# Whole 128x128 tiles for the router's flag sums, list products and spreads

## The chip, the cores and the metric

The kernel runs on one core of a Trainium2 chip. The metric is device time in microseconds (us), the median of three runs; a lower number is better. PE is the matrix engine (TensorE), PEld its weight load, DVE the vector engine, ACT the scalar engine, POOL the GpSimd engine, SP the engine that issues most DMAs.

## The reference, cut to what matters

Three layers run one after the other on 2176 tokens (4 batches of 512 local and 32 global positions) of 512 numbers each.

1. Attention, 8 heads of 64; global positions see everything, local ones a window of 32 to either side and the global ones.
2. A dense layer: `g = max(x @ w_in, 0) + alpha * min(x @ w_in, 0)`, then `g @ w_out` (512 to 2048 to 512).
3. A routed layer with 8 experts (512 to 1024 to 512), in which each expert takes exactly 2176 / 8 = 272 tokens. The assignment is greedy over all token and expert pairs:

```
logits = x @ w_gate
for idx in argsort(-logits.flatten()):
    tok, e = idx // 8, idx % 8
    if tok is taken or expert e has 272 tokens: continue
    give tok to e
out[tokens of e] = max(x[tokens of e] @ w1[e], 0) @ w2[e]
```

The change lies in the program of that assignment (the router) alone.

## The kernel before, in words

The three layers follow each other in time. PE's order is written out by hand in the dense layer's second half and in the experts (`manual_schedule`); the other engines' order is made by a planner when the program is built.

The router (`router`, `phase`, `listing`) does not sort. It closes one expert after the other, eight in all: `phase(k)` finds the threshold at which the next expert is full, and `listing(k)` makes the list of its 272 tokens (`IDS`), with which POOL later gathers their rows (`fetch_x`, tile `xg`). Tokens lie as 17 chunks (NT) of 128 partitions.

For seven of the eight experts `phase` takes six rounds. A round goes back and forth between PE and DVE:

- DVE compares the scores with 63 (first two rounds) or 31 thresholds (`against`, tile `gs`, 0 or 1).
- PE counts by thresholds and experts: `pc`, nine matmuls of 128 rows x 128 columns of weights (L886).
- DVE makes `lack` and the flags `sat` (L889, L891): 63 or 31 partitions by 8 experts.
- PE sums the flags over partitions and spreads the sum to all partitions: `pa`, one matmul with `ones` as weights over 63 or 31 rows (L898). This is the flag sum.
- DVE turns the sum into the next thresholds `th` (L901, L910) and goes on with `gs`.

At the end of a phase come `pq` (two matmuls of 128 rows by 128 columns, weights `late` and `ones`) and `pr` (one, weights `ones`, L965). The list of the expert before is made in the gaps of the next one's rounds: DVE builds `va` (tokens' numbers by 17 columns of the list) and `sb` (16 slots, at a pitch of 32), PE multiplies them with two chunks at a time: the list product `pl`, nine matmuls with 48 columns of weights and 68 moving columns (L831). DVE copies the two diagonal blocks to `lb` (L835), and one matmul with 64 rows, the spread `ps` (L838), brings them to all partitions.

PE does not stand still for this. Its matmuls are put between those of the dense layer's last product (`gemm2b`, L1174) and of the experts (`up`, L1047, and `down`, L1063), all in fp32 with 272 moving columns (tiles `h`). How many lie between two router steps is set by the constants WB, WA, WQ, WR and WL, in us of PE work, that the generators yield, and by `advance`, which counts them down. After `gemm2b`, PE gathers the first expert's tokens (`xt`) with filler matmuls (`idle`, L108) between. Expert weights come by DMA in pieces of 0.5 MB (`raw`, three buffers), ACT rounds each (L72) and POOL takes the rest (L73, tile `m`). `hh` and `hl` are the hidden layer in two parts, `xsh` and `xsl` the gathered tokens, `ot` an expert's result, `orow` its rows ahead of the scatter to the output.

Of the kernel before, what the change touches and what calls it, by code (L numbers as in the profile page):

```python
# [9 lines left out]
F32 = mybir.dt.float32  # L10
F32R = mybir.dt.float32r
BF = mybir.dt.bfloat16
# [3 lines left out]
OP = mybir.AluOpType  # L16
# [9 lines left out]
def tile_attention_moe_moe(ctx: ExitStack, tc: tile.TileContext, qkw, vw,  # L26
                           w_in, w_out, gate, w1, w2, out):
    nc = tc.nc
    V, A, P, T = nc.vector, nc.scalar, nc.gpsimd, nc.tensor
    B, H, S, D, SG = BHSDG  # L30
    DM, DF = w_in.shape
    E, _, FF = w1.shape
    NTOK = B * (S + SG)
    NT = NTOK // 128
# [274 lines left out]
    with ExitStack() as at:  # L309
# [299 lines left out]
        c = 0  # L609
# [31 lines left out]
    with tc.tile_pool(name="dc2", bufs=1, side="right") as dc, tc.tile_pool(name="pW", bufs=2, space=PSUM) as pW:  # L641
        more = []
        parts = [(win_part, i) for i in range(2 * KD)] + [(wout_part, i) for i in range(KH)]
        n = 0
# [22 lines left out]
    with ExitStack() as mo:  # L667
# [12 lines left out]
        LB = 16  # L680
# [36 lines left out]
        V.tensor_scalar(own, cols[:, :8].unsqueeze(1).to_broadcast([128, 3, 8]), pq_f[:, 0:1], None, op0=OP.is_equal)  # L717
        fr_b = rc_.tile([128, 128], I32, name="fr_b")
        V.tensor_scalar(fr_b, fr, LB - 1, None, op0=OP.bitwise_and)
        lb = rc_.tile([64, 2, 24], BF, name="lb")  # L720
        V.memset(lb, 0.0)
        spread = rc_.tile([64, 128], BF, name="spread")
        V.tensor_scalar(spread, fr_b[:64], pq_f[:64, 1:2], None, op0=OP.is_equal)
        ones = rc_.tile([128, 128], BF, name="ones")
        V.memset(ones, 1.0)
        one_c = rc_.tile([128, 2 * NT], F32, name="one_c")
# [32 lines left out]
        rp = rc_.tile([128, 2, E], F32, name="rp")  # L759
        V.memset(rp, float(CAP))  # L760
        ohs, gs, gi, vas, sbs = [], [], [0], [], []
        for i in range(2):
            ohs.append(rc_.tile([128, NT + 1, E], BF, name=f"ohs{i}"))
            P.memset(ohs[i], 0.0)
            gs.append(rc_.tile([128, NT + 1, 64], BF, name=f"gs{i}"))
            P.memset(gs[i], 0.0)
            vas.append(rc_.tile([128, NT + 1, LA, 2], BF, name=f"vas{i}"))
            P.memset(vas[i], 0.0)
            sbs.append(rc_.tile([128, NT + 1, 32], BF, name=f"sbs{i}"))
            P.memset(sbs[i], 0.0)  # L770
        Lrow = gx2.tile([128, LR], F32, name="Lrow")
        loadx(0, 1)
# [39 lines left out]
        def listing(k, pos):  # L812
            ra = rt.tile([128, NT], F32, name="ra")
            V.tensor_scalar(ra_h, pos, 1.0 / LB, -0.5 - 0.5 / LB, op0=OP.mult, op1=OP.add)
            V.tensor_scalar(ra, ra_h, MR, -MR, op0=OP.add, op1=OP.add)
            rb = rt.tile([128, NT], F32, name="rb")
            V.scalar_tensor_tensor(rb, ra, -float(LB), pos, op0=OP.mult, op1=OP.add)
            yield WL
            ha = rt.tile([128, NT, LA], BF, name="ha")
            V.tensor_tensor(ha, ra.unsqueeze(2).to_broadcast([128, NT, LA]),  # L820
                            col_h.unsqueeze(1).to_broadcast([128, NT, LA]), op=OP.is_equal)
            va, sb = vas[k % 2], sbs[k % 2]
            V.tensor_tensor(va[:, :NT], ha.unsqueeze(3).to_broadcast([128, NT, LA, 2]),
                            idc.unsqueeze(2).to_broadcast([128, NT, LA, 2]), op=OP.mult)
            yield WL
            V.tensor_tensor(sb[:, :NT, :LB], rb.unsqueeze(2).to_broadcast([128, NT, LB]),
                            slots.unsqueeze(1).to_broadcast([128, NT, LB]), op=OP.is_equal)
            yield WL
            pl = pm.tile([32 + LB, 2, LA, 2], F32, name="pl", tag="sm")
            for c in range(0, NT, 2):  # L830
                T.matmul(pl.rearrange("p c a t -> p (c a t)"), sb[:, c:c + 2].rearrange("p c l -> p (c l)")[:, :32 + LB],  # L831
                         va[:, c:c + 2].rearrange("p c a t -> p (c a t)"), start=c == 0, stop=c + 2 > NT)
            for i in range(2):
                r = slice(32 * i, 32 * i + LB)
                V.tensor_copy(lb[r, :, :LA], pl[r, i].rearrange("p a t -> p t a"))  # L835
            yield WL
            ps = pm.tile([128, 2, 3, 8], F32, name="ps", tag="sm")
            T.matmul(ps.rearrange("p t q a -> p (t q a)"), spread, lb.rearrange("p t a -> p (t a)"), start=True, stop=True)  # L838
            pk = rt.tile([128, 2, 3, 8], F32, name="pk")
            V.tensor_tensor(pk, ps, own.unsqueeze(1).to_broadcast([128, 2, 3, 8]), op=OP.mult)  # L840
            with nc.allow_low_precision(reason="whole numbers below 4096"):
                V.tensor_reduce(IDS[:, k], pk.rearrange("p t q a -> p q t a"), axis=AX.XY, op=OP.add)
            listed[0] = k + 1
            V.tensor_scalar(TT[:, :, k], ps[:, :, 2, 0], own[:, 0, k:k + 1], None, op0=OP.mult)
            if k == E - 1:
                with nc.allow_low_precision(reason="whole numbers below 4096"):
                    V.tensor_reduce(TID, TT.rearrange("p t e -> p (t e)"), axis=AX.X, op=OP.add)
# [22 lines left out]
        def phase(k, prev, v, mx, g):  # L870
# [8 lines left out]
            if not last:  # L879
                cur = None  # L880
                for i, s in enumerate(SH):
# [5 lines left out]
                                 ohw[:, c:c + 2].rearrange("p a e -> p (a e)"), start=c == 0, stop=c + 2 > NT)  # L887
                    lack = rt.tile([64, E], F32, name="lack")
                    V.tensor_tensor(lack[:n - 1], pc[64:63 + n, 1], rp[64:63 + n, 1], op=OP.subtract)  # L889
                    sat = rt.tile([64, E], BF, name="sat")  # L890
                    V.scalar_tensor_tensor(sat[:n - 1], pc[:n - 1, 0], -1.0, lack[:n - 1], op0=OP.mult, op1=OP.is_le)  # L891
                    if cur is not None:
                        n2 = (TH + [1])[i + 1]
# [1 line left out]
                        V.tensor_tensor(base[:, :n2], jt[i + 1], cur[:, 0:1].to_broadcast([128, n2]), op=OP.bitwise_xor)  # L895
                    yield WA[i]
                    pa = pm.tile([128, 64], F32, name="pa", tag="sm")
                    T.matmul(pa[:, :E], ones[:n - 1, :], sat[:n - 1], start=True, stop=True)  # L898
                    sj = sj_h
                    nf = rt.tile([128, 1], F32, name="nf")  # L900
                    V.tensor_scalar(sj, pa[:, :E], MF, 0.0, op0=OP.add, op1=OP.max, accum_out=nf)  # L901
# [463 lines left out]
```

## Time and profile before

| | |
|---|---|
| median of 3 runs | 867.75 us (864.87 to 870.67) |
| profiled execution | 866.48 us, its span 864.7 us |
| PE | busy 820.0 us (95%), 8380 matmuls |
| DVE | busy 467.2 us (54%) |
| ACT | busy 389.7 us (45%) |
| POOL | busy 348.6 us (40%) |
| chain that ended last | PE 73%, DVE 8%, issue 7%, ACT 5%, DMA 4%, POOL 3% |
| mean granted PE clock | 0.979 |

A share is an average over the whole span. The router's matmuls all start between 490 and 760 us, so it is there that the profile has to be read: by stretches, by the waits of PE inside them, and by the start times of single matmuls. A matmul's row gives its start and its length through the pipeline; since matmuls overlap, what one costs is seen in the distance between starts.

### The profile page before, as it was taken

The numbers are of one execution on the slowest core, as the hardware profiler recorded it, in microseconds if no ns is written. First come the engines' busy times: TensorE is split into PE (matmuls) and PEld (weight loads), VectorE is DVE, ScalarE is ACT, GpSimd is POOL, SyncE is SP. The second block draws the span as 40 slices with busy tenths as digits, with TensorE's granted clock in tenths as the row PEclk, the third lists the DMA queues.
The fourth block names the chain that finished last, engine by engine and source line by source line (L and its number), as shares of the span: only waits on it lengthen the run. The fifth ranks groups of instructions, "written<-read, shape, count | busy, mean of one in ns | idle before, by whom it ended". The sixth has DMA issues, their size and how long they took to land.

```text
span 864.7 us, 21014 instructions
## 1 busy us (share of the span) xinstructions
PE 820.0 (95%) x8380; PEld 748.4 (87%) x8380; DVE 467.2 (54%) x1654; ACT 389.7 (45%) x970; POOL 348.6 (40%) x299
## 2 busy tenths in 40 slices
PE   5789999999988999999999999999899999999995
PEld 3668788988988999898989899998689999899995
DVE  6789955364388734143333466766576776722120
ACT  5677656474455543332322434341254544454431
POOL 1124322020245534200000638370598868779601
PEclk9869999999999999999999999999999999999998
DMA  8965742631345302202211227242366655556300
GB/s 343 361 237 167 266 152 77 213 126 47 107 149 172 101 27 79 72 7 64 93 54 51 79 65 257 65 136 71 93 205 210 173 173 166 170 181 185 110 25 37
DMA packets 47993, 115.99 MB, mean 134 GB/s; under 512 B 4183, under 2 KB 20951, under 8 KB 45847
## 3 DMA queue, kind: packets, MB, share of 16 engines
q1 hardware_dynamic: 44999, 105.73, 37.9%
q0 software_dynamic: 2896, 8.92, 3.1%
q8 instruction: 66, 1.08, 0.5%
q14 instruction: 32, 0.26, 0.1%
HBM read 96.80 MB, written 17.83 MB: 133 GB/s over the span
## 4 chain that ended last, share of the span: by engine, by line
PE 73%; DVE 8%; issue 7%; ACT 5%; DMA 4%; POOL 3%; SPq 1%; POOLq 0%; ACTq 0%; DVEq 0%
PE h L191 20%; PE h L1174 12%; PE y L222 9%; PE h L1047 8%; PE h L1063 7%; PE o L422 3%; DVE mag L90 2%; PE lp L279 2%; DMA qk<-in_qk_dram 2%; PE go L471 2%; PE s L385 2%; POOL m L73 1%; PE t L411 1%; DMA raw<-in_moe_w_dram 1%; PE idle L108 1%
## 5 line engine op out<-in xcount | busy, mean ns | idle before, releaser
L191 PE MATMUL h<-xh,win 128*128 128x272 f32 x768 | 165.0, 298 | 3.5 <-DVE g L197 1.9
L73 POOL TENSOR_TENSOR m<-raw,m 128x1024 fp32r<-128x1024 f32 x64 | 152.3, 2403 | 22.0 <-ACT m L72 21.6
L191 PEld LDWEIGHTS h<-xh,win 128*128 128x128 f32 x768 | 126.5, 190 | 11.7 <-issue 4.1
L73 POOL TENSOR_TENSOR glo<-g,ghi 128x272 fp32r<-128x272 f32 x64 | 56.8, 890 | 142.8 <-ACT ghi L72 142.7
L222 PE MATMUL y<-ghi,wout 128*128 128x272 f32 x512 | 112.9, 298 | 1.4 <-ACT ghi L72 1.0
L191 PE MATMUL h<-xl,win 128*128 128x272 f32 x384 | 112.1, 293 | 0.5 <-DVE xl L73 0.5
L1174 PE MATMUL h<-gr,wout 128*128 128x272 f32 x768 | 110.7, 295 | 0.0
L73 POOL TENSOR_TENSOR gr<-gb,gr 128x272 fp32r<-128x272 f32 x64 | 48.0, 773 | 152.9 <-ACT gr L72 144.3
L1047 PE MATMUL h<-xsh,m 128*128 128x272 f32 x512 | 107.4, 297 | 1.1 <-ACT xsh L72 1.1
L1063 PE MATMUL h<-hh,m 128*128 128x272 f32 x512 | 103.3, 293 | 0.0
L1174 PEld LDWEIGHTS h<-gr,wout 128*128 128x128 f32 x768 | 99.2, 188 | 0.9 <-ACT gr L72 0.4
L196 ACT ACTIVATE neg<-h 128x272 f32<-128x272 f32 x128 | 50.5, 396 | 91.3 <-PE h L191 91.0
L222 PEld LDWEIGHTS y<-ghi,wout 128*128 128x128 f32 x512 | 84.2, 188 | 6.7 <-issue 3.4
L1047 PEld LDWEIGHTS h<-xsh,m 128*128 128x128 f32 x512 | 83.1, 190 | 2.3 <-ACT xsh L72 1.2
L1063 PEld LDWEIGHTS h<-hh,m 128*128 128x128 f32 x512 | 81.7, 188 | 0.7 <-issue 0.5
L72 ACT CAST m<-raw 128x1024 fp32r<-128x1024 f32 x64 | 65.3, 1048 | 26.7 <-DMA raw<-in_moe_w_dram 26.6
L1063 PE MATMUL h<-hl,m 128*128 128x272 f32 x256 | 75.5, 295 | 0.0
L1047 PE MATMUL h<-xsl,m 128*128 128x272 f32 x256 | 74.9, 293 | 0.5 <-issue 0.5
L222 PE MATMUL y<-glo,wout 128*128 128x272 f32 x256 | 73.7, 292 | 1.6 <-POOL glo L73 1.5
L191 PEld LDWEIGHTS h<-xl,win 128*128 128x128 f32 x384 | 73.2, 191 | 2.2 <-issue 1.0
L197 DVE SCALAR_TENSOR_TENSOR gb<-neg,al,h 128x272 f32<-128x272 f32 x64 | 31.7, 496 | 76.8 <-ACT neg L196 66.2
L393 ACT ACTIVATE pr<-sc,mx 128x128 f32<-128x128 f32 x128 | 50.0, 392 | 34.6 <-DVE mx L391 34.6
(230 smaller groups left out, 1513.5 us busy)
## 6 DMA issues: line engine op xcount, KB each, us to landing
raw<-in_moe_w_dram SPq DMA_DIRECT2D x64, 512.0 KB, 3.7
vv<-in_v_dram SPq DMA_DIRECT2D x16, 1024.0 KB, 7.8
qk<-in_qk_dram SPq DMA_DIRECT2D x14, 720.0 KB, 8.1
raw<-in_moe_w_in_dram SPq DMA_DIRECT2D x16, 512.0 KB, 6.4
raw<-in_moe_w_out_dram SPq DMA_DIRECT2D x16, 512.0 KB, 3.9
xs<-xb SPq DMA_DIRECT2D x16, 272.0 KB, 6.3
xpart<-xd SPq DMA_DIRECT2D x32, 136.0 KB, 3.7
xb<-xs SPq DMA_DIRECT2D x8, 544.0 KB, 3.9
```

The lines of the kernel that those rows point to most:

```text
L72: a = A.copy(hi, src)
L73: return a, (lo_eng or V).tensor_tensor(lo, src, hi.bitcast(F32), op=OP.subtract)
L90: V.scalar_tensor_tensor(bits, high, -0x40000000, bits, op0=OP.bitwise_and, op1=OP.bitwise_or)
L191: T.matmul(ps, wi[:, w, k, fs], x[:, k], start=i == 0, stop=i == 3 * KD - 1)
L196: A.activation(out=neg, in_=ps, func=AF.Relu, scale=-1.0)
L197: epi[0] = V.scalar_tensor_tensor(g, neg, al1[:, hf * KH + f:hf * KH + f + 1], ps, op0=OP.mult, op1=OP.add)
L222: T.matmul(ps, wo[:, w, f, ds_], x[:, f], start=i == 0, stop=i == 3 * KH - 1)
L393: A.activation(out=d["pr", j][:, ii], in_=sc, func=AF.Exp, bias=d["mx", j][:, ii:ii + 1], scale=-1.0, accum_out=d["sm", j][:, ii:ii + 1])
L422: T.matmul(o[c, a, WIN * ii:WIN * ii + WIN], U[2 * p + a]["v"][:, i, c], d["t", j][:, ii, lane(2 * a + h, i)], start=True, stop=True)
L1047: T.matmul(ps, d["w1"][:, w, kk, fs], x[:, kk], start=i == 0, stop=i == 3 * KD - 1)
L1063: T.matmul(ps, d["w2"][:, w, f, ms], x[:, f], start=i == 0, stop=i == 3 * K3 - 1)
L1174: T.matmul(ps[j], wo[:, w, f, ds_], x, start=f == 0 and a == 0, stop=f == KH - 1 and a == 2)
```

## The change

Three kinds of router matmuls get operands of full height and width.

- The flag sum `pa` runs over all 128 rows. `sat` is no longer a fresh tile of 64 partitions but one of two constant tiles of 128 (one for the rounds with 63 flags, one for those with 31), zeroed once; the rows above the flags stay zero.
- The list product takes four chunks at a time: five matmuls with 128 columns of weights and 136 moving columns, in place of nine with 48 and 68. `vas` and `sbs` are padded from 18 to 20 chunks. Four diagonal blocks, not two, are copied to `lb`.
- The spread `ps` runs over 128 rows; `spread` and `lb` have 128 partitions.

```diff
--- before.py
+++ after.py
@@ -717,10 +717,13 @@
         V.tensor_scalar(own, cols[:, :8].unsqueeze(1).to_broadcast([128, 3, 8]), pq_f[:, 0:1], None, op0=OP.is_equal)
         fr_b = rc_.tile([128, 128], I32, name="fr_b")
         V.tensor_scalar(fr_b, fr, LB - 1, None, op0=OP.bitwise_and)
-        lb = rc_.tile([64, 2, 24], BF, name="lb")
+        lb = rc_.tile([128, 2, 24], BF, name="lb")
         V.memset(lb, 0.0)
-        spread = rc_.tile([64, 128], BF, name="spread")
-        V.tensor_scalar(spread, fr_b[:64], pq_f[:64, 1:2], None, op0=OP.is_equal)
+        spread = rc_.tile([128, 128], BF, name="spread")
+        V.tensor_scalar(spread, fr_b, pq_f[:, 1:2], None, op0=OP.is_equal)
+        sats = [rc_.tile([128, E], BF, name=f"sat{i}") for i in range(2)]
+        for x in sats:
+            V.memset(x, 0.0)
         ones = rc_.tile([128, 128], BF, name="ones")
         V.memset(ones, 1.0)
         one_c = rc_.tile([128, 2 * NT], F32, name="one_c")
@@ -759,14 +762,15 @@
         rp = rc_.tile([128, 2, E], F32, name="rp")
         V.memset(rp, float(CAP))
         ohs, gs, gi, vas, sbs = [], [], [0], [], []
+        NP = -(-NT // 4) * 4
         for i in range(2):
             ohs.append(rc_.tile([128, NT + 1, E], BF, name=f"ohs{i}"))
             P.memset(ohs[i], 0.0)
             gs.append(rc_.tile([128, NT + 1, 64], BF, name=f"gs{i}"))
             P.memset(gs[i], 0.0)
-            vas.append(rc_.tile([128, NT + 1, LA, 2], BF, name=f"vas{i}"))
+            vas.append(rc_.tile([128, NP, LA, 2], BF, name=f"vas{i}"))
             P.memset(vas[i], 0.0)
-            sbs.append(rc_.tile([128, NT + 1, 32], BF, name=f"sbs{i}"))
+            sbs.append(rc_.tile([128, NP, 32], BF, name=f"sbs{i}"))
             P.memset(sbs[i], 0.0)
         Lrow = gx2.tile([128, LR], F32, name="Lrow")
         loadx(0, 1)
@@ -826,11 +830,11 @@
             V.tensor_tensor(sb[:, :NT, :LB], rb.unsqueeze(2).to_broadcast([128, NT, LB]),
                             slots.unsqueeze(1).to_broadcast([128, NT, LB]), op=OP.is_equal)
             yield WL
-            pl = pm.tile([32 + LB, 2, LA, 2], F32, name="pl", tag="sm")
-            for c in range(0, NT, 2):
-                T.matmul(pl.rearrange("p c a t -> p (c a t)"), sb[:, c:c + 2].rearrange("p c l -> p (c l)")[:, :32 + LB],
-                         va[:, c:c + 2].rearrange("p c a t -> p (c a t)"), start=c == 0, stop=c + 2 > NT)
-            for i in range(2):
+            pl = pm.tile([128, 4, LA, 2], F32, name="pl", tag="sm")
+            for c in range(0, NT, 4):
+                T.matmul(pl.rearrange("p c a t -> p (c a t)"), sb[:, c:c + 4].rearrange("p c l -> p (c l)"),
+                         va[:, c:c + 4].rearrange("p c a t -> p (c a t)"), start=c == 0, stop=c + 4 >= NT)
+            for i in range(4):
                 r = slice(32 * i, 32 * i + LB)
                 V.tensor_copy(lb[r, :, :LA], pl[r, i].rearrange("p a t -> p t a"))
             yield WL
@@ -887,7 +891,7 @@
                                  ohw[:, c:c + 2].rearrange("p a e -> p (a e)"), start=c == 0, stop=c + 2 > NT)
                     lack = rt.tile([64, E], F32, name="lack")
                     V.tensor_tensor(lack[:n - 1], pc[64:63 + n, 1], rp[64:63 + n, 1], op=OP.subtract)
-                    sat = rt.tile([64, E], BF, name="sat")
+                    sat = sats[n < TH[0]]
                     V.scalar_tensor_tensor(sat[:n - 1], pc[:n - 1, 0], -1.0, lack[:n - 1], op0=OP.mult, op1=OP.is_le)
                     if cur is not None:
                         n2 = (TH + [1])[i + 1]
@@ -895,7 +899,7 @@
                         V.tensor_tensor(base[:, :n2], jt[i + 1], cur[:, 0:1].to_broadcast([128, n2]), op=OP.bitwise_xor)
                     yield WA[i]
                     pa = pm.tile([128, 64], F32, name="pa", tag="sm")
-                    T.matmul(pa[:, :E], ones[:n - 1, :], sat[:n - 1], start=True, stop=True)
+                    T.matmul(pa[:, :E], ones, sat, start=True, stop=True)
                     sj = sj_h
                     nf = rt.tile([128, 1], F32, name="nf")
                     V.tensor_scalar(sj, pa[:, :E], MF, 0.0, op0=OP.add, op1=OP.max, accum_out=nf)
```

What comes when on PE stays as it was, but for the nine matmuls that become five. On DVE the planner's order moves in some places. Two of them:

DVE in the first expert's listing, during the second expert's fifth round (`gs` are the flags that PE's next count waits for), before:

```order
L901 TENSOR_SCALAR home,nf<-pa 128x8
L910 SCALAR_TENSOR_TENSOR th<-nf,home 128x32
L835 CAST lb<-pl 16x2x17 x2
L852 TENSOR_TENSOR gs_5403<-home,th 128x17x31
L917 SCALAR_TENSOR_TENSOR alive<-home,nf,alive 128x8
L1179 TENSOR_TENSOR pt<-h_7407,pt 128x272
```

The same place in the changed kernel:

```order
L905 TENSOR_SCALAR home,nf<-pa 128x8
L914 SCALAR_TENSOR_TENSOR th<-nf,home 128x32
L839 CAST lb<-pl 16x2x17 x3
L856 TENSOR_TENSOR gs_5407<-home,th 128x17x31
L921 SCALAR_TENSOR_TENSOR alive<-home,nf,alive 128x8
L839 CAST lb<-pl 16x2x17
L1183 TENSOR_TENSOR pt<-h_7403,pt 128x272
```

Three copies, not two, stand ahead of `gs`, and a fourth behind it.

DVE in the fifth expert's third round, at the end of the first expert's `down` on PE (`xsl` is made of the second expert's gathered tokens; `sat` is what PE's flag sum waits for), before:

```order
L889 TENSOR_TENSOR lack<-pc,rp 31x8
L895 TENSOR_TENSOR home<-home,th 128x32
L891 SCALAR_TENSOR_TENSOR sat<-pc,lack 31x8
L73 TENSOR_TENSOR xsl<-xt,xsh 128x4x128
L901 TENSOR_SCALAR home,nf<-pa 128x8
```

The same place in the changed kernel:

```order
L893 TENSOR_TENSOR lack<-pc,rp 31x8
L73 TENSOR_TENSOR xsl<-xt,xsh 128x4x128
L899 TENSOR_TENSOR home<-home,th 128x32
L895 SCALAR_TENSOR_TENSOR sat_5361<-pc,lack 31x8
L905 TENSOR_SCALAR home,nf<-pa 128x8
```

`sat` now stands behind `xsl`.

## Rows read from the trace of the kernel before

**Rows 1.** Page: the chain that ended last, shares of the span.

```profile
PE 73%; DVE 8%; issue 7%; ACT 5%; DMA 4%; POOL 3%; SPq 1%; POOLq 0%; ACTq 0%; DVEq 0%
```

**Rows 2.** Waits of PE, 485 to 757.5 us: total, times, longest (us).

```profile
PE pa L898 <- DVE sat L891: 0.5, 1, 0.5
```

**Rows 3.** Timeline of PE, one flag sum: start, length (us), matmul.

```profile
548.21 0.29 PE L1174 MATMUL h<-gr,wout 128*128 128x272 f32 x1
548.42 0.17 PE L898 MATMUL pa<-sat,ones 31*128 31x8 bf16 x1
...
548.76 0.42 PE L1174 MATMUL h<-gr,wout 128*128 128x272 f32 x2
```

**Rows 4.** Timeline of PE, one `pr`.

```profile
556.29 0.29 PE L1174 MATMUL h<-gr,wout 128*128 128x272 f32 x1
556.42 0.18 PE L965 MATMUL pr<-r,ones 128*128 128x8 bf16 x1
...
556.67 0.42 PE L1174 MATMUL h<-gr,wout 128*128 128x272 f32 x2
```

**Rows 5.** Timeline of PE, a flag sum with the list product behind it.

```profile
688.82 0.29 PE L1047 MATMUL h<-xsl,m 128*128 128x272 f32 x1
...
689.14 0.47 PE L831 MATMUL pl<-vas,sbs 128*48 128x68 bf16 x9
...
689.77 0.29 PE L1047 MATMUL h<-xsh,m 128*128 128x272 f32 x1
```

**Rows 6.** Timeline of PE, a flag sum with the spread behind it.

```profile
693.35 0.29 PE L1047 MATMUL h<-xsh,m 128*128 128x272 f32 x1
...
693.68 0.19 PE L838 MATMUL ps<-lb,spread 64*128 64x48 bf16 x1
...
694.03 0.29 PE L1047 MATMUL h<-xsl,m 128*128 128x272 f32 x1
```

**Rows 7.** Chain of waits, filler matmuls of 512 bf16 columns: start, length (us).

```profile
603.89 2.26 PE idle L108 x10
```

**Rows 8.** Windows, flag sums alone (L898): stretch, its length, PE busy (count).

```profile
485.00:602.00 117.00, 3.31 (x19) 1.73 (x19) 1.00 0.37 114
617.40:649.00 31.60, 0.88 (x5) 0.46 (x5) 1.00 0.60 182
649.00:743.70 94.70, 2.60 (x15) 1.36 (x15) 0.98 0.61 181
```

**Rows 9.** Windows: length, busy PE, PEld, DVE, ACT, POOL, clock, DMA, GB/s.

```profile
617.40:649.00 31.60, 29.67 (x261) 27.88 (x259) 23.24 (x96) 17.38 (x28) 28.84 (x15) 1.00 0.60 182
612.50:616.00 3.50, 3.50 (x22) 1.79 (x21) 1.69 (x4) 0.81 (x2) 0.00 (x0) 0.51 0.00 0
646.60:648.90 2.30, 0.69 (x6) 0.41 (x5) 2.20 (x8) 1.50 (x5) 2.15 (x2) 1.00 0.58 202
650.00:653.50 3.50, 3.50 (x26) 3.43 (x25) 0.75 (x3) 2.58 (x4) 3.18 (x3) 0.51 0.83 290
755.80:757.30 1.50, 0.27 (x3) 0.05 (x1) 1.47 (x4) 0.00 (x0) 1.47 (x2) 1.00 0.89 317
```

**Rows 10.** Chain of waits, in order of time: start, length (us), what.

```profile
609.19 2.17 issue
...
643.90 3.48 DMA raw<-in_moe_w_dram
...
749.20 3.78 DMA raw<-in_moe_w_dram
```

**Rows 11.** Timeline of DVE and PE after the first list product.

```profile
540.87 0.39 DVE L835 CAST lb<-pl 16x34 bf16<-16x34 f32 x2
541.29 0.71 DVE L852 TENSOR_TENSOR gs<-home,th 128x527 bf16<-128x527 f32 x1
...
542.87 0.38 PE L886 MATMUL pc<-ohs,gs 128*128 128x16 bf16 x9
543.11 0.37 PE L1174 MATMUL h<-gr,wout 128*128 128x272 f32 x1
```

## The prediction

> **What bounds the kernel now.** First the chain of waits: 73% of it is PE [rows 1], so the question for any part of this change is whether PE stands still there or works. The router runs between 490 and 760 us, so the waits of PE are read in that stretch. Of those that DVE causes at a flag sum there is one, of 0.5 us, among 42 sums [rows 2]: DVE nearly always has its flags ready before PE comes. In the long stretches PE is therefore the bound, and the router is paid for in PE time, as a detour between two matmuls of the main product.
>
> What a detour costs is read from starts, since lengths overlap. In the timeline of one flag sum, the last main matmul before it starts at 548.21 and the second after it at 548.76: 0.55 us [rows 3]. `pr` uses the same weights tile and the same 8 moving columns, but all 128 rows: 556.29 to 556.67, 0.38 us [rows 4]. The two kinds of matmul differ by 0.17 us, and the starts show where: PE enters `pa` 0.21 us after the main matmul and `pr` 0.13 us after it. So a matmul on part of the rows is charged at its borders with whole ones, and not for its own columns. All 42 sums are of the partial kind.
>
> Not everywhere does PE time count. Three places in which PE waits for something else are seen in the windows and the chain: 609 to 611 us, where the gather of the first expert waits 2.17 us for rows from memory [rows 10]; 646.6 to 648.9, where PE is busy 0.69 of 2.30 us and the chain comes over a weight DMA at 643.90, with POOL busy 28.84 of the 31.60 us before [rows 9, 10]; and 755.8 to 757.3, where PE is busy 0.27 of 1.50 us and the chain comes over a DMA at 749.20 [rows 9, 10]. PE time saved in the stretch that leads to such a wait makes the wait longer, and the end not earlier.
>
> **The change part by part.**
>
> *Flag sums.* 42 (six rounds, seven experts). Each becomes a matmul like `pr`: 0.55 - 0.38 = 0.17 us less [rows 3, 4]. By rows this is the change's largest term. Bounds: 0 if the difference is not one of rows (a rival, below), 0.17 if it is.
>
> *Spreads.* Eight. Six stand right behind a flag sum: 0.68 us for both [rows 6], so 0.13 more than the sum alone. Among whole tiles one more costs 0.03 us: nine `pc` and the step to the next main matmul take 542.87 to 543.11 [rows 11]. Saving 0.10 each. The two lone ones I price like a flag sum, 0.17.
>
> *List products.* Eight; six stand behind a flag sum, 0.95 us for both [rows 5], so 0.40 us for nine matmuls and their borders. The new one has five of 136 columns. The nearest row for its pitch is the filler: ten of 512 bf16 columns take 2.26 us [rows 7], so 136 columns take 0.06 and five take 0.30. Saving 0.10; for the two lone ones, which have both borders to themselves, 0.17 + 0.10 = 0.27. Here a rule speaks against the change. The rows show nine `pc`, each with its own load of 128 columns of weights, at 0.03 us a pair [rows 11]. The Trainium skill, "TensorE: Matmul & The Clock Gate", section "LDWEIGHTS (loading the stationary operand)", has the load's time grow with the columns of the weights, P / 1.2 ns. By that rule (an estimate from the page) 128 columns take 0.11 us in place of 0.04, and five loads 0.53 in place of nine's 0.36, so that the eight products would lose 1.4 us together instead of winning 1.1. The measured 0.03 us pair decides against it.
>
> *DVE.* Two more copies to `lb` per list, at 0.39 / 2 = 0.20 us: 16 in all, 3.1 us of DVE. One stands ahead of `gs`. There `gs` ends at 541.29 + 0.71 = 542.00 and PE comes at 542.87 [rows 11]: 0.87 us are free. The copy takes 0.20, and PE comes up to 0.27 earlier; 0.40 us stay. So nothing on PE's path. Where that cover is gone, it is 0.20 to 0.40 us for each of eight lists. `sat` behind `xsl` at 646 us delays a flag sum by up to a length of `xsl`; it falls in front of the 2.3 us in which PE waits anyway [rows 9], and I take 0 of a range of 0 to 0.7.
>
> *The rest.* The zeroed tiles and the four wider memsets come at the set-up, hundreds of us ahead of their use and beside main products; DMAs are neither added nor moved but for one POOL piece ahead of two gathers of `xg`, which are used some 15 us later. Nothing.
>
> *The sum by stretches* (the counts of flag sums in [rows 8]; the three between 602 and 617 are what is left of 42).
> - 485 to 602: 19 sums, 2 products, 2 spreads: 3.23 + 0.20 + 0.20 = 3.63, all on the path.
> - 602 to 617: two sums are beside the filler ahead of the 2.17 us wait and are hidden (0.34); one with a product behind the wait counts, 0.27.
> - 617 to 649: 5 sums and a spread, 0.95, hidden: POOL and the weight DMAs set the end of this stretch.
> - 649 to 744: 15 sums, 3 products, 3 spreads: 2.55 + 0.60 = 3.15, on the path.
> - 744 to 757: a lone product and a lone spread, 0.44, hidden in front of the wait at 755.8; those behind it, 0.44, count.
>
> On the path 3.63 + 0.27 + 3.15 + 0.44 = 7.49 us, hidden 1.73, together 9.22. A few rounds have no slack on DVE, as the flag sum that waits 0.5 us [rows 2]; in front of such a wait a saving is lost, at most 0.17 each, and I take off 0.4 for two or three of them. That leaves 7.1 us. The profiled execution took 866.48 us (span 864.7), so it would take 859.4. The median of the three runs is 1.27 higher, 867.75; less 7.1 that is 860.65, and I say **860.5**.
>
> **The rivals.**
>
> *The hidden part counts too.* The stretch to 649 is anchored at POOL and DMA, but PE's share in their order (a buffer that a matmul frees) could pull them along. For it: POOL is not busy all of the time. Against: PE's wait of 2.3 us just behind it [rows 9]. Then 9.2 us come off: 858.5.
>
> *Rows don't matter.* The difference between `pa` and `pr` would come from something else that always stands beside `pa`, and the change would not do what it says. Only the products' 0.10 us would be left, at seven of eight: 0.7, so 867. Against it speaks that `ps`, which waits for other work, carries the same border. The Trainium skill says so, though: in "TensorE: Matmul & The Clock Gate", section "Why this matters for your kernels", a single matmul on 32 rows takes the same time as one on 128. As long as only one matmul's own time is meant, the rows here agree; for the border they do not.
>
> *DVE takes some of it back.* If the slack of 0.87 us is thinner elsewhere, the two copies of all eight lists land on PE's path: 8 x 0.40 = 3.2 us. Then 7.1 - 3.2 = 3.9 us come off: 863.8.
>
> *The clock falls, and the kernel is slower.* PE comes earlier to three waits that stay: 2.17 us grow by 0.34, 2.30 by 0.95, 1.50 by 0.44. Behind the first two the granted clock is at half, 0.51 of full, for a stretch of about 3.4 us each [rows 9], and behind the third it is at full speed. Half speed for 3.4 us loses 1.7 us. If it fell behind the third too, and lasted three times as long behind the first two, that is 1.7 + 2 x 3.4 = 8.5 us, more than the 7.1: 867.75 + 1.4 = 869. It decides from the point at which about 14 us more are run at half clock. For it: the two waits that grow are those with a fall. Against: of the growing waits the longest is 3.3 us, not much above 2.3.
>
> **How the numbers follow.** The forecast has 0.60, the hidden part on top 0.15, rows don't matter 0.10, DVE 0.10, the clock 0.05. The forecast's own range is 858 to 863: 0.5 us for the places without slack, 0.7 for `xsl`, and about 1.5 for the run-to-run spread, which was 864.87 to 870.67. The range for 8 in 10 takes in the hidden part below and the DVE rival above: 857 to 865.5, leaving out rows and clock. What a measurement of this kernel can tell from no change is about 1%, 8.7 us, here 859.1. Faster by more: 0.12 from the first rival and 0.18 from the forecast's lower part, 0.30. Slower by more (above 876.4) needs twice the clock rival: 0.03. Within 1%: 0.67.
>
> **What would show it.** In the changed profile the distance from the last main matmul to the second after it is 0.38 at a flag sum (0.55 if rows don't matter), about 0.68 with a list product, 0.41 with a spread. The five list matmuls are 0.06 apart; 0.11 would give the rule on columns its due. The stretch from 485 us to the fillers is 3.6 us shorter, that of the first expert is not, and the wait at its end is about 1 us longer. New waits of PE for DVE `gs` behind a list product would show the DVE rival, more than two stretches at half clock the last one. The forecast is wrong if the border stays, or if a wait that I took for fixed moves.

## The result, and the profile after

| | before | the change |
|---|---|---|
| median | 867.17 us (863.07 to 870.67, 6 runs) | 857.48 us (856.2 to 860.98, 6 runs) |
| ratio | | 0.9898, 95% interval 0.9872 to 0.9925 |
| span of the profiled run | 864.7 us | 854.9 us |
| mean granted PE clock there | 0.979 | 0.985 |

Timed once more beside a later set of runs, the change had 861.43 us (11 runs) against 866.86 (16 runs), ratio 0.9931 (0.9908 to 0.9954). A gain of 0.75 to 0.92%, that is 6.5 to 8 us, lies in both intervals. The forecast was 860.5 us, 7.1 less than before, in a range of 857 to 865.5.

First the single detours of PE, the answer to [rows 3], [rows 5] and [rows 6]. The rows are from the timeline of PE in the changed kernel: start (us), length (us), matmul. A row at the end of each group is the second main matmul behind the burst.

```profile
544.55 0.29 PE L1178 MATMUL h<-gr,wout 128*128 128x272 f32 x1
544.68 0.18 PE L902 MATMUL pa<-sat,ones 128*128 128x8 bf16 x1
...
544.93 0.41 PE L1178 MATMUL h<-gr,wout 128*128 128x272 f32 x2
...
536.98 0.28 PE L1178 MATMUL h<-gr,wout 128*128 128x272 f32 x1
...
537.15 0.46 PE L835 MATMUL pl<-vas,sbs 128*128 128x136 bf16 x5
537.41 0.37 PE L1178 MATMUL h<-gr,wout 128*128 128x272 f32 x1
537.62 0.41 PE L1178 MATMUL h<-gr,wout 128*128 128x272 f32 x2
...
541.14 0.28 PE L1178 MATMUL h<-gr,wout 128*128 128x272 f32 x1
...
541.30 0.18 PE L842 MATMUL ps<-lb,spread 128*128 128x48 bf16 x1
...
541.53 0.41 PE L1178 MATMUL h<-gr,wout 128*128 128x272 f32 x2
```

A lone flag sum takes 544.55 to 544.93, 0.38 us (0.55 before); a sum with its list product 0.64 (0.95); a sum with a spread 0.39 (0.68). The five list matmuls and the step to the next main one lie between 537.15 and 537.41; the first two start at 537.15 and 537.21, 0.06 us apart, and the last step is shorter.

Now the stretches. The windows are cut at the same landmarks in both kernels: first and last matmul of the dense layer's last product, then the first matmul of `up` of experts 1, 2, 5 and 6. Columns as in [rows 9]. Before:

```profile
481.67:602.00 120.33, 118.57 (x1069) 113.45 (x1068) 77.24 (x322) 42.05 (x93) 65.86 (x71) 1.00 0.39 119
602.00:617.37 15.37, 12.67 (x85) 6.45 (x83) 8.45 (x30) 2.81 (x6) 3.33 (x4) 0.89 0.23 73
617.37:648.90 31.53, 29.60 (x260) 27.81 (x258) 23.17 (x96) 17.31 (x28) 28.77 (x15) 1.00 0.60 182
648.90:743.74 94.84, 93.46 (x825) 88.66 (x826) 64.77 (x283) 44.07 (x77) 74.17 (x41) 0.98 0.61 181
743.74:773.94 30.20, 28.81 (x236) 27.45 (x235) 12.84 (x50) 14.45 (x26) 23.80 (x14) 1.00 0.57 167
```

The changed kernel:

```profile
479.40:596.67 117.27, 114.98 (x1061) 111.95 (x1060) 78.06 (x326) 42.09 (x93) 66.05 (x71) 1.00 0.39 122
596.67:611.97 15.30, 12.21 (x80) 6.54 (x79) 8.42 (x30) 2.81 (x6) 3.32 (x4) 0.89 0.24 73
611.97:642.76 30.79, 28.81 (x261) 27.48 (x259) 23.38 (x97) 17.24 (x28) 28.72 (x15) 1.00 0.66 184
642.76:734.40 91.64, 89.36 (x814) 85.79 (x815) 65.80 (x289) 44.17 (x77) 74.10 (x41) 1.00 0.63 188
734.40:764.10 29.70, 28.13 (x229) 27.18 (x228) 13.53 (x54) 14.56 (x26) 23.81 (x14) 1.00 0.56 168
```

The first and the fourth stretch, in which PE is busy for 97% of the time or more, are 3.1 and 3.2 us shorter. The gather (602 to 617) has not moved, and the first expert's stretch went down by 0.7 us. Two things that are not the change stand in these numbers. The changed run came to the first landmark 2.3 us earlier (479.40 against 481.67), in front of all that was edited. And in the fourth stretch of before the clock was at half for 3.4 us [rows 9], in the profiled run of the change it was not (mean clock 0.98 and 1.00).

Of the waits of PE in the changed kernel (total us, times, longest) these are new or longer; before, `pr` waited 0.4 and `pa` 0.5. What is new at `pr` is one wait of 0.5 us in the first expert's stretch; `yt` stands in the dense stretch, `pa` and `pq` in experts 2 to 4:

```profile
PE pr L969 <- DVE r L964: 0.9, 2, 0.5
PE pa L902 <- DVE sat L895: 0.7, 1, 0.7
...
PE pq L949 <- DVE m L939: 0.5, 1, 0.5
PE yt L242 <- ACT yr L244: 0.4, 1, 0.4
```

### The profile page after: what moved, and what is told of

Its sections match the earlier page's. It is cut to its first block, busy times and chain, and to the rows that moved or that the text cites. A ratio compares the mean times of both kernels' runs of the same rounds, so it can differ in the third digit from the quotient of the medians.

```text
span 854.9 us, 20969 instructions
## 1 busy us (share of the span) xinstructions
PE 807.0 (94%) x8348; PEld 741.2 (87%) x8348; DVE 470.1 (55%) x1672; ACT 389.4 (46%) x970; POOL 348.8 (41%) x299
## 5 line engine op out<-in xcount | busy, mean ns | idle before, releaser
L1178 PE MATMUL h<-gr,wout 128*128 128x272 f32 x768 | 108.5, 294 | 0.0
```

The costliest lines, as they stand in the source:

```text
L1178: T.matmul(ps[j], wo[:, w, f, ds_], x, start=f == 0 and a == 0, stop=f == KH - 1 and a == 2)
```

## The experiments

Lengths of the five stretches in all profiled runs, worked out from the starts of the landmark matmuls; a star marks a fall to half clock for 3.4 us in the stretch. Kernels are in the order in which they are told below.

```
us                      dense   gather   expert 1  experts 2-4  expert 5
before                  120.32  15.38*   31.54     94.84*       30.20
before again            120.47  13.93    31.10     95.28*       30.04
change                  117.27  15.31*   30.78     91.64        29.69
change again            117.35  15.37*   31.46     92.70*       30.04
sums alone              117.81  15.29*   30.93     92.82*       30.13
lists alone             120.17  13.82    31.07     92.79        29.73
sums on 64 rows         120.31  13.81    30.63     93.02        29.63
96 rows, 112 columns    117.36  15.34*   30.72     92.16        29.79
65 rows, 80 columns     117.39  15.34*   31.60     92.52*       29.82
one copy per list       117.23  15.25*   30.20     91.63        29.89
more work ahead         117.35  13.75    31.48     91.81        29.20
16 filler pairs         117.39  13.83    31.12     92.62        27.80
third part as product   117.32  14.13    31.16     93.62*       28.99
third part turned       117.07  13.71    31.66     90.63        28.39
```

### Sums alone, lists alone

The flag sums whole, the lists as before:

```diff
-                    sat = rt.tile([64, E], BF, name="sat")
+                    sat = sats[n < TH[0]]
...
-                    T.matmul(pa[:, :E], ones[:n - 1, :], sat[:n - 1], start=True, stop=True)
+                    T.matmul(pa[:, :E], ones, sat, start=True, stop=True)
```

> Only the flag sums are made whole (128 rows, constant zeroed tiles); list products and spreads stay as before. Theory (a matmul on part of the array is charged at its borders with whole ones): a lone flag sum falls from 0.55 to 0.38 us between the last main matmul and the second after it; the six sums with a product and the six with a spread behind them gain less than that, since the burst still holds a partial matmul. Of the 30 lone ones 24 lie where PE is the bound, so about 24 x 0.17 - 0.4 = 3.7 us off: near 863.5 where before is 867.2. Rival (the border comes from something else that goes with the flag sum, not from its rows): 0.55 stays, no gain, 867.

The other half of the diff (list products, `lb`, `spread`), the flag sums as before:

> Only list products (five of 128 columns) and spreads (128 rows) are made whole; the flag sums stay at 63 and 31 rows. Theory: a lone flag sum stays at 0.55 us, sum with product about 0.85 (0.95 before), sum with spread about 0.58 (0.68 before), lone product and spread fall by 0.27 and 0.17; in time about 1.5 us off. Together with the run that makes only the sums whole this gives less than the whole change's 9 us, because in the twelve mixed bursts the border goes only when all of the burst is whole. Rival (weight loads cost by their columns, 0.11 us each): sum with product 1.0 or more, and 0 to 1 us slower than before.

Sums alone: 860.91 us against 867.01, ratio 0.9934 (0.9904 to 0.9964), 3 to 8 us off where 3.7 were expected. A lone sum has 0.38 us, as the median of those between two main matmuls; a sum with a product 0.86, with a spread 0.59, so both kept 0.2 of their border. Lists alone: 861.64 us, ratio 0.9936 (0.9907 to 0.9965); distances 0.56, 0.81 and 0.58 us, near what was expected. The time was not: 1.5 us were expected. The stretches show that this kernel's dense part is as long as before (120.17), and that its profiled run has neither of the two falls of the clock. Its runs had a mean clock of 0.983, those of before beside them 0.9786. So the rival on weight loads fell here as well (0.81 is below 0.95, not above it), and the size in time of this half is left open between 1.5 us, which the distances give, and 5.5, which its runs had.

By their times the halves together (6.1 and 5.4 us) give more than the whole change (9.7, later 5.4), and not less, as was expected. In the dense stretch, which repeats best, they do give less: 2.6 and 0.2 us, where the change gives 3.1.

### Sums on 64 rows

The change with one line different:

```diff
-                    T.matmul(pa[:, :E], ones, sat, start=True, stop=True)
+                    T.matmul(pa[:, :E], ones[:64, :], sat[:64], start=True, stop=True)
```

> The whole change, but the flag sum runs over the first 64 rows of the same constant tiles instead of 128; DVE's work and every other instruction are the same. Theory (rows): the lone flag sum is back at 0.55 us, and the time back by the 35 visible sums x 0.17 = 6 us, about 863 to 865. Rival (what saved time was the constant tile, or the order of DVE that comes with it): 0.38 us and the time of the change, 857.5.

864.0 us against 867.01, ratio 0.9975 (0.9945 to 1.0005): most of the gain is gone, as the theory had it. The timeline of one flag sum, as above:

```profile
550.59 0.29 PE L1178 MATMUL h<-gr,wout 128*128 128x272 f32 x1
550.80 0.18 PE L902 MATMUL pa<-sat,ones 64*128 64x8 bf16 x1
...
551.14 0.42 PE L1178 MATMUL h<-gr,wout 128*128 128x272 f32 x2
```

PE enters the sum 0.21 us after the main matmul, and the whole is 0.55 us. The instructions of PE, DVE, ACT and POOL and their order are those of the change. It is the rows.

### How many rows are enough

Flag sums on 96 rows and list products with 112 columns of weights; then sums on 65 rows and products of three chunks with 80 columns, in place of whole tiles (the second one's edit, cut to its main lines):

```diff
-                    T.matmul(pa[:, :E], ones, sat, start=True, stop=True)
+                    T.matmul(pa[:, :E], ones[:65, :], sat[:65], start=True, stop=True)
...
-            pl = pm.tile([128, 4, LA, 2], F32, name="pl", tag="sm")
-            for c in range(0, NT, 4):
+            pl = pm.tile([80, 3, LA, 2], F32, name="pl", tag="sm")
+            for c in range(0, NT, 3):
...
```

> The change, but with tiles that are nearly whole: flag sums over 96 of the 128 rows, list products with 112 of the 128 columns of weights. Read from the profile alone, by distances. Theory (what counts is whole or not): a lone flag sum is back at 0.55 us, a lone list product loses 0.1 to 0.2 against the 0.63 or so of whole tiles in a sum-and-product burst. Rival (the charge grows with the share that is left out, or 96 rows and 112 columns count as whole): 0.38 to 0.45 us and no loss.

> The change with tiles just over half: flag sums over 65 of 128 rows, list products three chunks at a time with 80 of 128 columns of weights and 102 moving columns (six matmuls). 64 rows paid the full border, 96 rows and 112 columns paid none. Theory (the charge falls where a matmul fits half of the array, 64 rows or columns): 0.38 us for a lone flag sum, near 0.65 for a sum with product. Rival (the border lies higher, between 65 and 96 rows or 80 and 112 columns): 0.55 and 0.75 or more.

Each was run once (861.33 and 863.03 us), so they are read by their distances. On 96 rows a lone sum takes 0.38 us as the median, and a sum with a product of 112 columns 0.67 (0.64 for 128): the theory written for this run, that only whole tiles are free, fell. The second run put the border where its own theory had it. The timelines: a lone sum on 96 rows, then of the second run a lone sum, and a sum with a product.

```profile
548.08 0.29 PE L1178 MATMUL h<-gr,wout 128*128 128x272 f32 x1
548.21 0.18 PE L902 MATMUL pa<-sat,ones 96*128 96x8 bf16 x1
...
548.46 0.42 PE L1178 MATMUL h<-gr,wout 128*128 128x272 f32 x2
...
548.83 0.29 PE L1178 MATMUL h<-gr,wout 128*128 128x272 f32 x1
548.96 0.18 PE L902 MATMUL pa<-sat,ones 65*128 65x8 bf16 x1
...
549.20 0.42 PE L1178 MATMUL h<-gr,wout 128*128 128x272 f32 x2
...
541.23 0.28 PE L1178 MATMUL h<-gr,wout 128*128 128x272 f32 x1
...
541.39 0.45 PE L835 MATMUL pl<-vas,sbs 128*80 128x102 bf16 x6
...
541.87 0.41 PE L1178 MATMUL h<-gr,wout 128*128 128x272 f32 x2
```

65 rows: 0.37 us. 80 columns: 0.64. One row above half of the array is as good as all of it; 64 rows, and 48 columns, pay. Between 48 and 80 columns nothing was run. The Trainium skill, "TensorEngine Tiling (Array Packing)", section "Key Properties", says that a change of tiling mode drains the engine, and its section "Available Configurations" has modes of 64 and of 32 rows, and none between 64 and 128. The traces agree with both: 0.17 us more, at 64 rows and not at 65. That the 0.17 us are such a drain, no run shows by itself.

### One copy per list

```diff
-            for i in range(4):
-                r = slice(32 * i, 32 * i + LB)
-                V.tensor_copy(lb[r, :, :LA], pl[r, i].rearrange("p a t -> p t a"))
+            V.tensor_copy(lb[:, :, :, :LA], pl.rearrange("p c a t -> p c t a"))
...
+            for i in range(4):
+                T.matmul(ps.rearrange("p t q a -> p (t q a)"), spreads[:, i], lb[:, i].rearrange("p t a -> p (t a)"), start=i == 0, stop=i == 3)
```

> The change, with less DVE work per list: one copy of the whole 128 by 136 product to lb in place of four copies of its blocks, and four spreads of 128 rows in place of one, each with the weights of one block of rows. DVE loses about 0.5 us per list, PE gains three whole matmuls, 3 x 0.03 us. Theory that DVE takes back part of the change's gain (its copies stand ahead of the flags that PE waits for): up to 1 to 3 us faster than the change. Rival (DVE's slack covers the copies, as the prediction has it): within 1 us of the change, 857 to 859, and the waits of PE for DVE stay the same within 0.5 us in sum.

858.41 us, ratio 0.9912 (0.9885 to 0.994), no different from the change. A sum with its four spreads takes 0.48 us in place of 0.40. The dense stretch and the fourth are 117.23 and 91.63 (117.27 and 91.64 in the change), and the waits for DVE stay: `pr` 1.1 us, `pa` 0.7, `pc` 0.6 (0.9, 0.7 and 0.5 in the change). The copies are not what PE waits for.

### More work ahead of two steps

```diff
-        WQ, WR0, WR, WL = 2.7, 6.0, 4.2, 1.2
+        WQ, WR0, WR, WL = 3.1, 6.0, 4.8, 1.2
...
-        NB0 = 12
+        NB0 = 16
```

> The change with 16 filler pairs and with more main PE work ahead of two router steps: 3.1 in place of 2.7 ahead of the matmuls on the kept tokens (pq) and 4.8 in place of 4.2 ahead of the count of what is left (pr). In the change's profile PE waits 0.9 us for DVE at pr and 0.5 at pq; before it was 0.4 and 0. Theory (the change's shorter bursts brought PE to DVE's results too early, and that is where part of the gain between 640 and 735 us went): these waits go, and the three experts' stretches are 1 to 1.4 us shorter in sum than the change's 91.6; 1 to 1.5 us faster in time. Rival (the wait moves to the next router step, since DVE's chain per expert is what takes the time): the sum of waits for DVE stays and so does the time.

857.26 us, ratio 0.9893 (0.9869 to 0.9916); the change beside it 861.43. The waits of PE in its profile:

```profile
PE h L1051 <- ACT xsh L72: 2.3, 1, 2.3
PE pa L902 <- DVE sat L895: 1.7, 2, 1.0
PE ox L1098 <- ACT orow L1099: 1.5, 3, 0.7
PE xt L1037 <- issue: 0.6, 1, 0.6
```

The waits at `pr` and `pq` are gone, that at `pa` has risen from 0.7 to 1.7 us, that for `orow` from 0.3 to 1.5. Experts 2 to 4 take 91.81 us, no less than the change's 91.64. The rival has it: the wait moved on. This kernel also has the 16 filler pairs, and the kernel with these alone (next section) is as fast: 856.6 us, ratio 0.99. By the profiles it even takes 0.6 us less over experts 2 to 5 (120.4 against 121.0). So the added work has no gain of its own; what this kernel has over the change goes with the fillers, in the gather (13.75 us, no fall of the clock) and behind it.

### Filler ahead of the gather

The edit is the line on NB0 above, alone.

> The change, with 16 in place of 12 pairs of filler matmuls ahead of the first expert's gather, so that PE works through most of its 2.6 us wait for rows from memory. Theory (the half clock that follows in some profiles, 3.4 us of it, comes of that wait; it is where the prediction saw part of the gain hidden): no half clock behind this wait, the stretch from the last dense matmul to the first expert's first is 13.8 us as in the profiles without the fall, in place of 15.3: 1.5 us faster than the change's runs that had it. Rival (the fall does not depend on that wait, or the fillers push the gather back): the stretch stays at 15.3 or grows.

856.6 us, ratio 0.99 (0.9876 to 0.9925). The gather is 13.83 us, without a fall. The change's windows of the wait and of what follows, and this kernel's whole gather:

```profile
603.30:606.04 2.74, 0.19 (x1) 0.03 (x1) 0.82 (x4) 0.00 (x0) 1.99 (x3) 1.00 0.53 121
606.80:610.30 3.50, 3.50 (x20) 1.89 (x19) 1.39 (x4) 1.17 (x2) 0.00 (x0) 0.51 0.04 11
```

```profile
600.36:614.19 13.83, 12.98 (x100) 7.05 (x98) 9.89 (x36) 3.06 (x6) 3.58 (x4) 1.00 0.26 81
```

In the change PE is idle for 2.55 of 2.74 us and then runs 3.5 us at 0.51 of its clock; with four more pairs it stays at full clock. But four kernels without them (before again, lists alone, sums on 64 rows, the next one's product) had no fall behind the same wait either. With 16 pairs none of three profiles has it; with 12, seven of eleven. The length of the wait goes with it: PE waited 2.46 to 2.62 us in the two profiles of the change and in four variants (sums alone, 96 rows, 65 rows, one copy), and all six have the fall; it waited 2.07 to 2.20 us in the other five, and one has it (before, 2.17). The change makes this wait longer by 0.4 us. That it thereby brings on the fall more often is what these few profiles suggest; they do not show it.

The fillers do one more thing. While they run, the router goes on: one flag sum, one spread and nine `pc` more lie in the gather than in the change, and one list product comes up from expert 5's stretch into experts 2 to 4. So the stretches behind the gather are not like for like here; experts 2 to 5 together take 120.4 us, in the change 121.3.

### The third part of the gather

The last 16 tokens of each expert are transposed on 16 rows, a partial matmul that the change left. First as a product with 16 columns of the identity over a zeroed tile of 128 rows; then, with the 16 filler pairs, as a whole transpose (both cut to the line on PE):

```diff
+                    if q < 2:
                         T.transpose(t[:, kk, :n], d["xg"][:n, q, kk * 128:(kk + 1) * 128], ident[:n, :n])
+                    else:
+                        T.matmul(t[:, kk, :n], XG3[0][:, kk * 128:(kk + 1) * 128], ident[:, :n], start=True, stop=True)
```

```diff
-                        T.matmul(t[:, kk, :n], XG3[0][:, kk * 128:(kk + 1) * 128], ident[:, :n], start=True, stop=True)
+                        T.transpose(t[:, kk], XG3[0][:, kk * 128:(kk + 1) * 128], ident)
```

> The change, and besides the third part of each expert's gather (16 tokens, four transposes on 16 rows) is made whole: the 16 rows are gathered into a zeroed tile of 128 partitions and multiplied with 16 columns of the identity over all 128 rows. Theory (any partial matmul pays the border): the burst, 0.79 us from the last main matmul to the second after it, falls to about 0.45; six or seven of the eight are on PE's path, so about 2 us faster than the change: 855.5. Rival (only bf16 matmuls of the router pay, or the wait for the rows of the gather takes it back): no difference from the change, 857.5.

> The change with 16 filler pairs, and the third part of the gather as a transpose over all 128 rows and 128 columns (the tile is zeroed above its 16 rows), not as a product with 16 columns of the identity, which had split into eight matmuls and eaten what the border gave. A whole transpose takes 0.109 us a step, four take 0.44; so the burst should be 0.13 + 0.44 + 0.03 + 0.21 less the first step, about 0.66 us, in place of 0.79. Theory (fp32 transposes on 16 rows pay the border like the router's bf16): 0.66 us, and near 1 us faster than the change with 16 pairs alone (856.6). Rival (they pay something else, or whole transposes cost more than the border): 0.79 or above and no gain.

The product: 859.8 us, ratio 0.9927 (0.9895 to 0.9959), no gain over the change. The transpose: 856.12 us in 4 runs, ratio 0.9874 (0.9839 to 0.9909), the lowest median of all, but no different from the 16 pairs alone (0.99). The same burst (of expert 8) in the change, as a product, and as a whole transpose:

```profile
817.82 0.29 PE L1067 MATMUL h<-hh,m 128*128 128x272 f32 x1
818.03 0.41 PE L1037 MATMUL xt<-ident,xg 16*128 16x16 f32 x4
...
818.61 0.41 PE L1067 MATMUL h<-hh,m 128*128 128x272 f32 x2
```

```profile
819.41 0.29 PE L1071 MATMUL h<-hh,m 128*128 128x272 f32 x1
819.54 0.96 PE L1041 MATMUL xt<-ident,xg 128*128 128x16 f32 x8
...
820.56 0.41 PE L1071 MATMUL h<-hh,m 128*128 128x272 f32 x2
```

```profile
818.12 0.29 PE L1071 MATMUL h<-hh,m 128*128 128x272 f32 x1
818.26 0.60 PE L1041 MATMUL xt<-ident,xg 128*128 128x128 f32 x4
...
818.82 0.41 PE L1071 MATMUL h<-hh,m 128*128 128x272 f32 x2
```

0.79 us, 1.15 us, 0.70 us. In both edits PE enters at 0.13 to 0.14 us in place of 0.21, so the border is gone. But here an fp32 product runs as two matmuls each (x8, not x4), 0.8 us in all. My expectation overlooked that. The whole transposes save 0.09 us a burst, not the 0.13 that were expected, and the near 1 us of gain does not show in the time.

### Before and the change once more

> The kernel before once more, unchanged, for a second profile. Theory: the length of each stretch between landmarks on PE comes back within 0.3 us, but for the falls of the clock (1.5 us each) and the stretch of the first expert, whose end hangs on weight DMAs. If the first expert's stretch is again 31.5 us, its 0.4 to 0.9 us less in all changed kernels is a gain of the change; if it is below 31, it is scatter.

> The change once more, unchanged, beside the others: a second profile of it and more times. Theory (7 us by the mean of the granted clock taken out, and more by luck of the clock in its first runs): nearer 859 to 860 than 857.5 against 866 before. Rival (the change also takes away falls of the clock behind its shorter waits): 857.5 again, at a mean granted clock of 0.982 to 0.983 against 0.979 before.

The second profile of before gave 120.47 us for the dense stretch and 31.10 for the first expert's, the second of the change 117.35 and 31.46. So the dense stretch repeats within 0.15 us and its 3.1 us are the change's; the first expert's scatters by 0.4 to 0.7 us and has no gain that can be told from that. Experts 2 to 4 of before came back 0.44 us longer (94.84 and 95.28, both with the fall), more than the 0.3 that were expected. The one time of before here, 862.35 us, is that of the profiled run. The time of the change came out at 861.43 us, above what either theory had, at a mean clock of 0.9797 over its runs (0.9827 in the first six; before, 0.979). So the clock that the rival needed, 0.982 to 0.983, did not come back. Over all timed runs, with a constant for each kernel, 0.001 of mean clock goes with 0.44 us; with that taken out the two measurements give 7.4 and 5.1 us, each good to 1.2 to 1.6.

The clock is not all of the scatter. The two profiled runs of the change are 7.1 us apart (854.9 and 862.0), at 0.985 and 0.983, and 4.7 us of that lie ahead of the first landmark, which PE reaches at 479.40 and 484.13 us. Over all profiles it is reached at 478.0 to 484.8 us, though no edit touches what comes before it.

## Why the prediction was right, point by point

**The border between partial and whole matmuls.** It rested on one pair of rows, `pa` against `pr`, and it held: 0.38 us measured for 0.38 forecast, and 0.55 again when only the rows were taken back to 64. The sum with a product came to 0.64 (0.68 forecast), with a spread to 0.39 (0.41). "Partial" was too wide a word: on rows the charge stops one row above half of the array.

**The products' pitch and the rule on columns.** Forecast 0.06 us from start to start, measured 0.06 (0.26 for all five with the step to the next main matmul). The rule of the Trainium skill, "TensorE: Matmul & The Clock Gate", section "LDWEIGHTS (loading the stationary operand)", would have had 0.11 (an estimate from the page); the measurement decides against it for these bf16 loads.

**The dense stretch.** 3.63 us forecast, of PE's work. PE's busy time there went from 118.57 to 114.98, 3.59 us less; the stretch is 3.1 us shorter. The difference, 0.5 us, is new idle time, 0.4 of it a wait for ACT's copy of the rows ahead (`yt` for `yr`). Before, PE did not wait there at all; with the sums alone and the lists alone, which bring it there less early, it waited 0.1 us.

**Experts 2 to 4.** 3.15 us forecast. With the fall of the clock in both, 95.1 us (mean of two profiles of before) became 92.7 and 92.5 (the change again, and 65 rows): 2.4 to 2.6 us. PE's busy time fell from 93.46 to 90.64 where both have the fall, 2.8 us; its idle time rose from 1.4 to 2.1. The window of the change's second profile, columns as above:

```profile
648.31:741.01 92.70, 90.64 (x814) 87.21 (x814) 65.99 (x288) 44.09 (x77) 74.03 (x41) 0.98 0.62 185
```

**What was hidden.** 0.95 us in the first expert's stretch were taken as lost, and the stretch's mean over two profiles went from 31.3 to 31.1. PE's busy time there fell by 0.8 us (29.60 and 29.61 to 28.81 and 28.76), and by the means most of it came back as idle time. But not where the forecast had it: the wait at the stretch's end did not grow by 1 us (1.6 and 1.3 us before with the `xt` ahead of it, 0.9 and 1.3 in the change); `pr` in the middle took 0.5 and 1.4 us. The two flag sums ahead of the gather's wait were taken as lost, 0.34 us: the wait grew from 2.17 and 2.20 to 2.55 and 2.62, and the stretch, with the fall in both, went from 15.38 to 15.31 and 15.37. The 0.27 us behind that wait did not show. The rival that the hidden part counts, which gives 858.5, is not borne out by the stretches, though the first six runs lie near it.

**The places without slack, the mis-sized term.** I took off 0.4 us. The idle time that came up is 0.5 us in the dense stretch and 0.7 in experts 2 to 4, about 1.2 in all (0.6 in each by the means of two profiles). Over the five stretches, with falls of the clock in the same places, the change takes off 3.1 + 0 + 0.2 + 2.5 + 0.2 = 6.0 us, where 7.1 were forecast. The mechanism was of the DVE rival's kind, PE coming to results before they are there, but not by its copies: one copy in place of four changed nothing. In the dense stretch it was not DVE at all but ACT's copy. In experts 2 to 4 it is DVE (`pa` 0.2 more in both profiles, `pq` 0.5 in the first alone), and more work ahead of `pq` and `pr` only moved the wait. That the round of DVE work per expert begins to bound there fits this, but no run shortened that round, so it is argued and not shown. The size of the rival (3.2 us) was not reached.

**The number, and luck.** The range held both medians, but the first (857.48) only just, and they lie 9.7 and 5.4 us below before where the stretches give 6.0. Of the 7.1 us between the two profiled runs of the change 4.7 lie ahead of all that was edited. So a median near 860.5 could not have borne out the sum; the single distances and the dense stretch do, for its largest term.

**The other rivals.** That rows don't matter fell with the run on 64 rows. Of the clock rival one part came true: behind the gather's wait, which grew, the fall stands in both profiles of the change and in one of the two of before, and it takes 1.4 us (13.93 us without it and 15.38 with it, before). No fall behind these waits was longer than 3.4 us, none came behind the last wait, and the one behind the first expert was there in both profiles of before and in one of the change. So the time did not come out near that rival's 869.

## What to carry to other kernels

Where small matmuls are threaded between full ones, compare in the timeline the distance between the main matmuls around a small one of 64 rows or fewer with that around a small one of more: a constant zeroed tile can buy the difference, here 0.17 us for each flag sum, with no instruction more on the other engines while the router runs. Count only those in stretches where the engine does not wait at the end. And when the bound engine gets faster by a per cent, take off for the partners' slack: here nearly a fifth of the PE time saved in the two long stretches (1.2 of 6.4 us) came back as waits that were not there before.

## What the runs showed of the hardware that I had not expected

- 65 rows or 80 columns cost what 128 cost (0.37 and 0.64 us), 64 rows the full border (0.55): a step, not a slope.
- An fp32 product against a piece of the identity ran as eight matmuls where a transpose of the same tile ran as four: 1.15 us against 0.70, for an eighth of the moving columns.
- The same kernel's median differed by 4 us between two sets of runs (857.48 and 861.43), with the mean clock at 0.9827 and 0.9797. By the 0.44 us for 0.001 the clock goes with 1.3 of these.
- Behind the same wait of the gather PE's clock fell to half for 3.4 us in one profile of before (wait 2.17 us) and not in the other (2.20).
